# One slot per buffer, slack in the planner's ready times, and a new order for a linear-attention and two-MLP kernel

## The chip, the cores and the metric

One core of one Trainium2 chip runs the whole program in one launch. The metric is the device time of one execution in microseconds (us); lower is better. TensorE (PE) multiplies matrices, VectorE (DVE), ScalarE (ACT) and GpSimd (POOL) do the elementwise work, SyncE (SP) issues nearly all DMAs. Each engine works its own list of instructions in the order in which the program was written, and waits on semaphores where another engine or a DMA must come first.

## The reference, cut to what matters

```python
# q, k, v: (4, 8, 576, 64); w_phi: (64, 128); all float32
def phi(x):
    proj = np.einsum('bhsd,df->bhsf', x, w_phi)
    proj = proj - np.max(np.abs(proj), axis=-1, keepdims=True)
    return np.concatenate([np.exp(proj), np.exp(-proj)], axis=-1)
q_p, k_p = (phi(q), phi(k))
kv = np.einsum('bhsf,bhsd->bhfd', k_p, v)
z = np.sum(k_p, axis=2)
attn = np.einsum('bhsf,bhfd->bhsd', q_p, kv) / (np.einsum('bhsf,bhf->bhs', q_p, z)[..., None] + 1e-06)
x = attn.transpose(0, 2, 1, 3).reshape(2304, 512)
h = x @ w_in                        # (512, 2048)
x = (h * sigmoid(h)) @ w_out        # first MLP, (2048, 512)
h = np.maximum(x @ w_in2, 0.0)
out = (h * h) @ w_out2              # second MLP
```

## The kernel before

The program has three stages on PE. **Attention** goes by batch `j` (0 to 3) and pair of heads `p` (0 to 3): `keys_of` projects the keys, takes exponentials and builds the 129-row table `kv`; `queries_of(b, p)` does the same for half a batch of queries (`b`, 0 to 7), multiplies with `kv`, sends the denominators through DRAM to spread them over partitions (`rr`, `rd`, `qb`, three DMAs in a row) and writes the normalised result, split in a high and a low part, into the tiles `x`. **The first MLP** takes tokens in six pieces `i` (288, 288, four of 432 columns) and hidden units in 16 chunks `c`: `chunk(i, c)` makes 12 matmuls into a PSUM bank `h`, then ACT (`a`), DVE (`a`), ACT (`gh`) and DVE (`gl`) turn it into the gate, and 12 matmuls add to the four outputs `o`. Its weights come as raw 1 MB loads `wbits`; ACT and DVE make them float32 (`wc`, three instructions) and split them in high and low halves (`w`). Chunks in `STREAM` are stored to `w1d` and fetched again for every later piece. The second MLP's weights are converted in the same way during pieces 3 to 5: 32 loads `wr`, 32 conversions `wc` through the two slots of pool `c`, 32 stores to `w2d`. **The second MLP** works by Strassen-like products: `quad` (PE into `pa`, `pb`, `pc`) and `fold` (PE into `y`), with weights made by `w_sums` and `y_ahead`.

Nothing of this is issued in the order of the code. Each piece of work is recorded by `op(key, engine, cost, ...)`, and `Plan.run` (L176 to L265) plays the program through with its own costs: on every engine the ready operation with the smallest `key` starts, a DMA takes a fixed issue time, a latency and a rate (L84), an operation becomes ready at the end of its last input plus an entry of `LAT` (L260). The order in which operations start in this play is the order in which they are emitted. The numbers in `KEYS` (L290) shift the keys of whole groups: when weights are loaded, when queries of a batch come, and so on. Buffers are counted by pool (`self.free`), and a tile is allocated when its first operation is emitted, from a pool with one tag and several `bufs`; only five pools carry a slot number (`homes`, a heap that gives the lowest free number), and there it only chooses between two memory regions. Where the play leaves PE idle for more than 1.9 us in the attention, `idle_mm` puts in small matmuls (L1563, L1573).

Of the kernel before, what the change touches and what calls it, by code (L numbers as in the profile page):

```python
# [75 lines left out]
class Plan:  # L76
# [3 lines left out]
        "PE": {"ACT": 200, "DVE": 200, "POOL": 280, "SP": 250}, "ACT": {"DVE": 142, "PE": 170, "POOL": 200, "SP": 140},  # L80
        "DVE": {"ACT": 120, "PE": 150, "POOL": 170, "SP": 120}, "POOL": {"ACT": 135, "DVE": 135, "PE": 150, "SP": 150},
# [94 lines left out]
    def run(self):  # L176
# [9 lines left out]
        while left:  # L186
            moved = True
            while moved:
                moved = False
# [47 lines left out]
            while events and events[0][0] <= now:  # L237
# [5 lines left out]
                for b in o.frees:  # L243
                    b.users -= 1
                    if not b.users:
                        self.free[b.pool] += 1
                        if b.pool in self.homes:
                            heapq.heappush(self.homes[b.pool], b.home)
                        if b.pool in self.last:
                            last = self.last[b.pool]  # L250
# [50 lines left out]
def attention_then_two_mlps(ctx, tc, kT, qT, v, w_phi, w1, w2, out):  # L301
# [69 lines left out]
    def slot(name, unit, shape=(128, S), dt=F32):  # L371
        if unit.early:
            return Buf("e", lambda: ep[0].tile(list(shape), dt, tag="t", name=name), unit)
        b = Buf("t", None, unit)

        def make():
            if b.home < NT:
                return tp.tile(list(shape), dt, tag="t", bufs=NT, name=name)
            late_pool()
            return ep[2].tile(list(shape), dt, tag="t", bufs=NTL, name=name)  # L380
# [18 lines left out]
    def g_tiles(late, dts, name):  # L399
        return Buf(  # L400
            late or "g",
            lambda: [
                (late_pool() if late else gp).tile([128, LB], dt, tag=t, bufs=1 if late else 2, name=t + name)
                for t, dt in zip(("a", "gh", "gl"), dts)
            ], None
        )

    def wide(pool_, shape, dt, name):
        b = Buf(pool_, None, None)

        def make():
            wide_pool()
            if pool_ == "x7":
                return [
                    [late_pool().tile([128, w], dt, tag=t, bufs=1, name=name + t)[:, :QB] for t, w in (("gl", LB), ("xx", QB))],
                    [cp.tile([128, QB], dt, tag="c", bufs=2, name=f"{name}c{x}") for x in range(2)],
                ]
            if pool_ == "xt":
# [10 lines left out]
            return [sp.tile([128, LB], dt, tag="o", bufs=2, name=f"{name}{x}") for x in range(2)]  # L429
# [58 lines left out]
    blank_u = Buf("e", lambda: ep[0].tile([128, 256], F32, tag="t", name="zeros"), None)  # L488
    blank_ps = Buf("eb", lambda: psb.tile([128, 512], F32, tag="b", name="warm"), None)
# [63 lines left out]
    def w_tile(layer, c, turn=0):  # L553
        if (layer, c, turn) not in wch:
            shape, dt = [128, 4, 512], F32R
            if layer in (1, 3) and c < 2:
                wch[layer, c, turn] = Buf(
                    "wl", lambda: wide_pool().tile([128, 8, 256], F32R, tag="w", bufs=2, name=f"wl{layer}_{c}"), None
                )
# [6 lines left out]
            wch[layer, c, turn] = Buf(  # L566
                "w" if first else "wq",
                lambda: (wp if first else late_pool()).tile(
                    shape, dt, tag="w", bufs=NC - NW if first else NWQ, name=f"w{layer}_{c}_{turn}"
                ), None  # L570
# [1053 lines left out]
```

## Time and profile before

| what | value |
|---|---|
| median of 3 runs (961.84 to 964.12) | 962.52 us |
| the profiled execution, its own time | 966.88 us |
| its span from the first to the last instruction | 965.1 us |
| PE busy in the span | 936.1 us, 97% |
| DVE, ACT, POOL busy | 655.4, 558.3, 149.7 us |
| DMA traffic | 175.86 MB, mean 182 GB/s |
| chain that ended last, by engine | PE 70%, DMA 13%, DVE 10%, ACT 4% |

The page gives busy time by engine over the whole span and in 40 slices; the windows view gives the same for stretches of one's choice; the chain is followed back from the last instruction, at each step to what released it. A wait is put down to the semaphore that came last.

### The profile page before, as it was taken

How to read it: one execution, taken by the hardware profiler on the slowest of the kernel's cores; microseconds unless marked ns; L12 is line 12 of the kernel's file. 1: busy time of each engine (PE TensorE's matmuls, PEld its weight loads, DVE VectorE, ACT ScalarE, POOL GpSimd, SP SyncE). 2: the span in 40 equal slices, each digit the busy share in tenths (PEclk: the TensorE clock that was granted, in tenths of full speed). 3: DMA queues.
4: the chain of work that ended last, by engine and by line, in shares of the span. 5: the costliest groups of instructions: out<-in, count | busy, mean ns of one | idle time of the engine just before them, and what ended most of it. 6: DMA issues, size and time to landing. Idle time of an engine off the chain costs nothing.

```text
span 965.1 us, 16758 instructions
## 1 busy us (share of the span) xinstructions
PE 936.1 (97%) x6210; PEld 896.5 (93%) x6210; DVE 655.4 (68%) x1137; ACT 558.3 (58%) x1191; POOL 149.7 (16%) x160
## 2 busy tenths in 40 slices
PE   9889999999999999999999999999999999999998
PEld 7569999999999999988899899999999999999998
DVE  6889996646754477547554855757466799897952
ACT  7967786777766567434333554546565675444431
POOL 4210230200400203000001333511100430000000
PEclk9989999999999999999999999999999999999999
DMA  9769537344353145798878563444237574544422
GB/s 322 228 226 341 192 111 209 99 147 155 103 160 122 33 149 173 235 315 263 294 276 280 180 251 105 170 166 164 108 126 247 197 284 134 173 133 118 156 78 66
DMA packets 83954, 175.86 MB, mean 182 GB/s; under 512 B 14880, under 2 KB 43680, under 8 KB 77216
## 3 DMA queue, kind: packets, MB, share of 16 engines
q1 hardware_dynamic: 83728, 174.72, 54.7%
q8 instruction: 49, 0.80, 0.3%
q14 instruction: 33, 0.27, 0.1%
q10 hardware_dynamic: 144, 0.07, 0.0%
HBM read 126.11 MB, written 48.57 MB: 181 GB/s over the span
## 4 chain that ended last, share of the span: by engine, by line
PE 70%; DMA 13%; DVE 10%; ACT 4%; issue 2%; SPq 1%; DVEq 0%; ACTq 0%
PE y L1420 17%; PE h L1080 13%; PE o L1119 13%; PE pb L1248 7%; DMA w2d<-wc 5%; PE pa L1248 5%; PE pc L1248 5%; PE pkv L843 4%; PE pn L999 3%; DMA qb<-rd 2%; DMA qr<-qT 1%; DVE wc L537 1%; DVE w L449 1%; PE pk L775 1%; ACT wc L528 1%
## 5 line engine op out<-in xcount | busy, mean ns | idle before, releaser
L1080 PE MATMUL h<-x,w 128*128 128x432 f32 (+1 forms) x1152 | 214.2, 339 | 4.9 <-ACT x L445 2.1
L1119 PE MATMUL o<-gh,w 128*128 128x432 f32 (+1 forms) x768 | 209.7, 340 | 1.8 <-ACT gh L445 1.8
L1080 PEld LDWEIGHTS h<-x,w 128*128 128x128 f32 x1152 | 197.6, 189 | 12.8 <-ACT x L445 2.3
L1119 PEld LDWEIGHTS o<-gh,w 128*128 128x128 f32 x768 | 140.0, 188 | 7.6 <-ACT gh L445 3.1
L1119 PE MATMUL o<-gl,w 128*128 128x432 f32 (+1 forms) x384 | 130.9, 341 | 3.9 <-DVE gl L449 3.9
L947 POOL PARTITION_ALL_REDUCE qm<-qp x32 | 71.7, 2266 | 176.5 <-ACT qp L940 139.7
L1119 PEld LDWEIGHTS o<-gl,w 128*128 128x128 f32 x384 | 72.1, 188 | 9.6 <-DVE gl L449 7.5
L449 DVE TENSOR_TENSOR gl<-a,gh 128x432 fp32r<-128x432 f32 (+1 forms) x96 | 56.9, 593 | 29.9 <-ACT gh L445 29.0
L648 POOL TENSOR_TENSOR ws<-ws 128x256 f32<-128x256 f32 x52 | 48.5, 934 | 155.9 <-DVE w L449 103.2
L445 ACT CAST gh<-a 128x432 fp32r<-128x432 f32 (+1 forms) x96 | 49.5, 516 | 38.4 <-DVE a L1088 37.9
L1088 DVE SCALAR_TENSOR_TENSOR a<-a,h 128x432 f32<-128x432 f32 (+1 forms) x96 | 52.7, 549 | 26.1 <-ACT a L1084 25.7
L1084 ACT ACTIVATE a<-h 128x432 f32<-128x432 f32 (+1 forms) x96 | 47.4, 493 | 21.4 <-PE h L1080 21.3
L535 DVE TENSOR_SCALAR wc<-wc 128x512 int32<-128x512 int32 (+1 forms) x48 | 25.8, 537 | 43.8 <-ACT wc L528 43.5
L528 ACT ACTIVATE wc<-wr 128x512 f32<-128x512 f32 x32 | 21.3, 666 | 51.3 <-DMA w2d<-wc 43.1
L843 PE MATMUL pkv<-v,kd 128*128 128x128 f32 x256 | 49.6, 275 | 0.8 <-issue 0.8
L843 PE MATMUL pkv<-v,ke 128*128 128x128 f32 x256 | 49.5, 275 | 0.0
L965 ACT ACTIVATE qe<-qp 128x576 f32<-128x576 f32 x64 | 41.8, 686 | 9.1 <-DVE qp L953 8.8
L449 DVE TENSOR_TENSOR qo<-qe,qh 128x576 fp32r<-128x576 f32 x48 | 37.9, 800 | 11.7 <-ACT qh L445 10.8
L1420 PE MATMUL y<-yb,w 128*128 128x256 f32 x316 | 44.3, 279 | 1.4 <-DVE yb L449 1.4
L999 PE MATMUL pn<-qh,kv 128*65 128x288 f32 x192 | 42.4, 295 | 0.6 <-ACT qn L1002 0.6
L1420 PEld LDWEIGHTS y<-yb,w 128*128 128x128 f32 x316 | 40.1, 188 | 1.6 <-DVE yb L449 1.6
L843 PEld LDWEIGHTS pkv<-v,kd 128*128 128x128 f32 x256 | 39.5, 192 | 1.9 <-issue 1.0
(373 smaller groups left out, 2278.6 us busy)
## 6 DMA issues: line engine op xcount, KB each, us to landing
w<-w1d SPq DMA_DIRECT2D x30, 1024.0 KB, 5.6
wbits<-w SPq DMA_DIRECT2D x16, 1024.0 KB, 7.9
wr<-w SPq DMA_DIRECT2D x32, 512.0 KB, 5.2
fold<-gd SPq DMA_DIRECT2D x32, 512.0 KB, 3.9
gd<-g SPq DMA_DIRECT2D x24, 384.0 KB, 2.3
w2d<-wc SPq DMA_DIRECT2D x32, 256.0 KB, 5.3
qr<-qT SPq DMA_DIRECT2D x56, 144.0 KB, 4.3
ws<-w2d SPq DMA_DIRECT2D x26, 256.0 KB, 4.6
```

Source lines behind the costliest of these rows:

```text
L445: nc.scalar.copy(out=dst, in_=src)
L449: e.tensor_tensor(out=dst, in0=src, in1=hi.bitcast(F32), op=ALU.subtract)
L648: nc.gpsimd.tensor_tensor(out=get(f)[:, o], in0=get(f)[:, a], in1=get(f)[:, b], op=how)
L843: nc.tensor.matmul(get(ps)[:, o:o + 128], feats[a](s)[:, t], get(vt)[:, c:c + 128], start=t == 0 and a == 0 and s == 0, stop=False, skip_g ...
L947: nc.gpsimd.partition_all_reduce(get(mx), get(pr).rearrange("p a t -> p (a t)"), 128, bass.bass_isa.ReduceOp.absmax)
L999: nc.tensor.matmul(get(ps)[:D1, :HB], w, get(e)[:, t], start=x == 0, stop=x == len(ops) - 1)
L1080: nc.tensor.matmul(get(ps)[:, :cols], a, x[:, cc, :cols], start=k == 0, stop=k == 3 * ND - 1)
L1084: nc.scalar.activation(out=get(gb)[0][:, :cols], in_=get(ps)[:, :cols], func=AF.Tanh, scale=0.5)
L1088: nc.vector.scalar_tensor_tensor(out=a, in0=a, scalar=1.0, in1=get(ps)[:, :cols], op0=ALU.add, op1=ALU.mult)
L1119: nc.tensor.matmul(get(acc)[:, :cols], a, g[:, :cols], start=c == 0 and x == 0, stop=c == NC - 1 and x == 2)
L1248: nc.tensor.matmul(get(ps)[:, :QB], ws[a][:, f], row(b, y, cc), start=first and k == 0, stop=k == 5, skip_group_check=True,)
L1420: nc.tensor.matmul(get(acc)[:, d * 256:d * 256 + half], get(ws[a][0])[:, ws[a][1], s], both(y)[:, j], start=q == 0 and d == 0 and x == 0, ...
```

## The change

Three things are changed. **Slots.** Every pool now has a queue of slot numbers (a `deque`); planning takes the slot at the front and puts a freed one at the back, so a buffer gets the slot that has been free the longest, and the tile is made under a tag of its own (`t3`, `b5`) with `bufs=1`. PSUM banks get numbers in the same way. **Slack.** An operation that waits for another engine becomes ready later in the play: by `md` = 524 ns after a DMA, `mp` = 304 ns where PE waits for another engine, `me` = 50 ns otherwise; nothing is added on one and the same engine, and `LAT` has new entries for ACT and DVE with themselves. **Order.** All numbers of `KEYS` are others; `bx` goes from 8 to 6, which moves two more pairs of keys (6 and 7) to the form in which ACT makes the exponential out of PSUM with a bias, without the subtraction on DVE, and `nwr` from 4 to 2, the number of chunks by which a raw weight load may run ahead of the split. The program has the same matmuls but for four more `idle_mm` ones, six subtractions fewer on DVE, 30 instructions more on ACT (36 small exponentials from PSUM and 6 negations for 12 exponentials of whole groups), and ten more stores of `gd`, since more of its tiles lie in two parts.

```diff
     LAT = {
-        "PE": {"ACT": 200, "DVE": 200, "POOL": 280, "SP": 250}, "ACT": {"DVE": 142, "PE": 170, "POOL": 200, "SP": 140},
-        "DVE": {"ACT": 120, "PE": 150, "POOL": 170, "SP": 120}, "POOL": {"ACT": 135, "DVE": 135, "PE": 150, "SP": 150},
+        "PE": {"ACT": 200, "DVE": 200, "POOL": 280, "SP": 250}, "ACT": {"ACT": 115, "DVE": 142, "PE": 170, "POOL": 200, "SP": 140},
+        "DVE": {"DVE": 122, "ACT": 120, "PE": 150, "POOL": 170, "SP": 120}, "POOL": {"ACT": 135, "DVE": 135, "PE": 150, "SP": 150},
...
-        self.homes = {p: list(range(32)) for p in ("t", "xt", "gq", "fx", "rb")}
+        self.homes = {p: deque(range(n)) for p, n in pools.items()}
+        self.opened = dict(pools)
...
-                        if b.pool in self.homes:
-                            b.home = heapq.heappop(self.homes[b.pool])
+                        b.home = self.homes[b.pool].popleft()
...
-                        if b.pool in self.homes:
-                            heapq.heappush(self.homes[b.pool], b.home)
+                        self.homes[b.pool].append(b.home)
...
-                    a.ready = max(a.ready, now + self.LAT[o.engine].get(a.engine, 20 if a.engine == "ACT" else 0))
+                    slack = KEYS["md"] if o.engine == "SP" else KEYS["mp"] if a.engine == "PE" != o.engine else KEYS["me"]
+                    if o.engine == a.engine:
+                        slack = 0
+                    a.ready = max(a.ready, now + self.LAT[o.engine].get(a.engine, 0) + max(0, slack))
...
 KEYS = {
-    "k0s": 15.71, "q0s": 16.3, "q0": 9.87, "w0": 53.89, "ws": 10.28, "we": -9.07, "Q1": 45.24, "A1": 1.22, "Q2":
...
+    "k0s": 19.81, "q0s": 16.62, "q0": 10.46, "w0": 164.39, "ws": 74.59, "we": -0.62, "Q1": 44.46, "A1": -7.97,
...
+    "ss": 32.21, "md": 524, "mp": 304, "me": 50,
...
-        return Buf(pool_, lambda: psb.tile([128, 512], F32, tag="b", name=name), unit)
+        b = Buf(pool_, None, unit)
+
+        def make():
+            home, base = b.home, {"eb": 0, "acc": 0, "att": 4, "h": 4 + NATT}
+            opens = plan.source["pb"] if pool_ == "pb" else ()
+            at = base[opens[home]] + opens[:home].count(opens[home]) if opens else base[pool_] + home
+            return psb.tile([128, 512], F32, tag=f"b{at}", bufs=1, name=name)
...
+    def homed(pool_, name, where, shape, dt, tag, unit=None):
+        b = Buf(pool_, None, unit)
+        b.make = lambda: where().tile(list(shape), dt, tag=f"{tag}{b.home}", bufs=1, name=name)
+        return b
...
-            f = Buf("c", lambda: cp.tile([128, cols], F32, tag="c", name="wc" + n), None)
+            raw = homed("raw", "wr" + n, lambda: rp, (128, 2 * cols), I32, "raw")
+            f = homed("c", "wc" + n, lambda: cp, (128, cols), F32, "c")
```

Three places show the new order. The names end in numbers: `qb0_2` is block 0, pair 2; `w0_5` chunk 5 of the first MLP; `wc1_2_1` chunk 2, second half, of the second MLP's weights.

SP before the first chunk of the first MLP, before:

```order
L1025 DMA qb0_1_546<-rd_101 64x576
L1016 DMA rr0_2_550<-qn0_2_514 96x1x6
L522 DMA wbits_7_0_576<-w1 128x2048
L1025 DMA qb1_0_596<-rd_101 64x576
L1016 DMA rr0_3_599<-qn0_3_583 96x1x6
L597 DMA w1d_99<-w0_4_0_585 128x2048
L1022 DMA rd_101<-rr0_2_550 96x6
L1022 DMA rd_101<-rr0_3_599 96x6
L1016 DMA rr1_1_659<-qn1_1_635 96x1x6
L1025 DMA qb0_2_663<-rd_101 64x576
L1025 DMA qb0_3_674<-rd_101 64x576
```

The same place on SP in the change:

```order
L1037 DMA qb0_0_498<-rd_101 64x576
L1028 DMA rr0_2_500<-qn0_2_486 96x1x6
L1037 DMA qb0_1_520<-rd_101 64x576
L541 DMA wbits_4_0_539<-w1 128x2048
L1028 DMA rr0_3_542<-qn0_3_529 96x1x6
L541 DMA wbits_5_0_565<-w1 128x2048
L1034 DMA rd_101<-rr0_2_500 96x6
L1034 DMA rd_101<-rr0_3_542 96x6
L1028 DMA rr1_0_610<-qn1_0_589 96x1x6
L1037 DMA qb0_2_615<-rd_101 64x576
L1037 DMA qb0_3_629<-rd_101 64x576
```

The raw load `wbits_7` stands ahead of `qb0_3` before, `wbits_5` is the last one there now; of block 1 `rr1_0`, `rr1_1` and `qb1_0` stood ahead of it before, `rr1_0` alone now.

DVE around the last two normalisations of block 0 (`x0_2`, `x0_3`), before:

```order
L449 TENSOR_TENSOR w0_5_0_671<-wc0_5_0_548,w0_5_0_671 128x2x512
L1041 TENSOR_TENSOR x0_2_690<-qn0_2_514,qb0_2_663 64x288 x2
L1019 RECIPROCAL rr1_1_659<-rr1_1_659 96x6
L1041 TENSOR_TENSOR x0_3_695<-qn0_3_583,qb0_3_674 64x288 x2
L449 TENSOR_TENSOR x_0_533<-x0_2_690,x_0_533 128x288
```

The same place on DVE in the change:

```order
L468 TENSOR_TENSOR w0_2_0_537<-wc0_2_0_502,w0_2_0_537 128x2x512
L468 TENSOR_TENSOR w0_3_0_563<-wc0_3_0_527,w0_3_0_563 128x2x512
L965 TENSOR_TENSOR qp1_3_608<-qp1_3_608,qm1_3_631 128x576
L1031 RECIPROCAL rr1_0_610<-rr1_0_610 96x6
L1053 TENSOR_TENSOR x0_2_654<-qn0_2_486,qb0_2_615 64x288 x2
L1053 TENSOR_TENSOR x0_3_662<-qn0_3_529,qb0_3_629 64x288 x2
L468 TENSOR_TENSOR x_0_569<-x0_2_654,x_0_569 128x288
```

Six weight splits (`w0_0` to `w0_5`) are written ahead of `x0_2` before, four (`w0_0` to `w0_3`) now.

ACT in piece 4 of the first MLP, before:

```order
L445 CAST gh4_2_5424<-a4_2_5423 128x432
L528 ACTIVATE wc1_1_1_5444<-wr1_1_1_5329 128x512
L528 ACTIVATE wc1_2_1_5472<-wr1_2_1_5351 128x512
L528 ACTIVATE wc1_3_1_5495<-wr1_3_1_5428 128x512
L1084 ACTIVATE a4_3_5510<-h4_3_5478 128x432
L445 CAST gh4_3_5511<-a4_3_5510 128x432
L1084 ACTIVATE a4_4_5535<-h4_4_5497 128x432
L445 CAST gh4_4_5536<-a4_4_5535 128x432
L1084 ACTIVATE a4_5_5545<-h4_5_5521 128x432
L528 ACTIVATE wc1_4_1_5552<-wr1_4_1_5458 128x512
```

ACT in the same piece in the change:

```order
L547 ACTIVATE wc1_4_1_5726<-wr1_4_1_5675 128x512
L1096 ACTIVATE a4_10_5734<-h4_10_5713 128x432
L464 CAST gh4_10_5735<-a4_10_5734 128x432
L464 CAST x_5_5063<-x7_2_5771 128x288
L547 ACTIVATE wc1_5_1_5779<-wr1_5_1_5738 128x512
L1096 ACTIVATE a4_11_5786<-h4_11_5756 128x432
L464 CAST gh4_11_5787<-a4_11_5786 128x432
L1096 ACTIVATE a4_12_5820<-h4_12_5802 128x432
L547 ACTIVATE wc1_6_1_5832<-wr1_6_1_5781 128x512
```

Three conversions in a row stood between two chunks' gates; now there is one per chunk, and the 32 of them begin some four chunks later and reach from chunk 8 of piece 3 to chunk 12 of piece 5 (before: to chunk 14 of piece 4). PE's own list went from groups of three (three `h`, then three `o`) to one `h` and one `o` in turn, and the last block of queries (`b` = 7) from piece 3 into piece 4.

## Rows read from the trace of the kernel before

**Rows 1.** The page: the span, and PE's busy time.

```profile
span 965.1 us, 16758 instructions
...
PE 936.1 (97%) x6210; PEld 896.5 (93%) x6210; DVE 655.4 (68%) x1137; ACT 558.3 (58%) x1191; POOL 149.7 (16%) x160
```

**Rows 2.** Windows: length, busy time per engine, PE clock, DMA share, GB/s.

```profile
0.00:25.00 25.00, 22.84 (x166) 18.00 (x168) 16.64 (x26) 19.59 (x42) 9.80 (x18) 1.00 0.92 322
25.00:50.00 25.00, 20.39 (x135) 14.74 (x136) 20.52 (x30) 21.93 (x42) 6.95 (x9) 0.95 0.72 229
50.00:75.00 25.00, 20.93 (x128) 16.66 (x127) 22.56 (x38) 16.93 (x31) 2.59 (x7) 0.85 0.68 230
75.00:100.00 25.00, 25.00 (x216) 24.43 (x215) 24.40 (x44) 18.60 (x34) 0.45 (x6) 1.00 0.98 329
100.00:150.00 50.00, 49.57 (x381) 48.74 (x380) 46.45 (x73) 42.04 (x87) 13.64 (x6) 1.00 0.41 138
...
400.00:450.00 50.00, 47.90 (x240) 44.59 (x240) 30.59 (x62) 19.62 (x41) 0.00 (x0) 1.00 0.87 292
450.00:500.00 50.00, 47.98 (x241) 44.66 (x240) 26.88 (x50) 19.47 (x36) 0.00 (x0) 1.00 0.77 261
500.00:550.00 50.00, 47.71 (x239) 44.29 (x238) 30.30 (x45) 23.42 (x41) 10.74 (x11) 1.00 0.73 246
550.00:600.00 50.00, 50.00 (x258) 48.02 (x259) 30.17 (x45) 22.69 (x41) 17.41 (x22) 1.00 0.49 173
...
750.00:800.00 50.00, 46.94 (x321) 46.21 (x320) 43.05 (x66) 32.26 (x61) 18.96 (x19) 1.00 0.66 232
```

**Rows 3.** The chain that ended last, 30 to 60 us: start, us, what.

```profile
34.31 5.66 DMA rd<-rr
...
39.98 8.30 DMA qb<-rd
...
50.51 1.72 DVE qp L953
...
53.01 2.29 ACT qe L965 x4
...
55.35 3.90 DMA qb<-rd
```

**Rows 4.** Timelines of PE and ACT in the same stretch: start, us, [idle before <-releaser].

```profile
22.84 2.10 PE L999 MATMUL pn<-qe,kv 128*65 128x288 f32 x8
...
41.91 2.25 PE L999 MATMUL pn<-qe,kv 128*65 128x288 f32 x8 [1.67 <-ACT kv L858]
...
64.13 0.41 ACT L1084 ACTIVATE a<-h 128x288 f32<-128x288 f32 x1 [1.02 <-PE h L1080]
```

**Rows 5.** Groups by line, 0 to 100 us: busy us, mean ns.

```profile
L537 DVE SCALAR_TENSOR_TENSOR wc<-wbits,wc 128x1024 int32<-128x1024 int32 x13 | 15.9, 1223 | 0.4
...
L449 DVE TENSOR_TENSOR w<-wc,w 128x1024 fp32r<-128x1024 f32 x11 | 13.6, 1238 | 2.5 <-ACT w L445 2.5
...
L805 DVE TENSOR_TENSOR kd<-pk,mx 128x512 f32<-128x512 f32 (+1 forms) x21 | 11.5, 556 | 0.5
...
L535 DVE TENSOR_SCALAR wc<-wc 128x1024 int32<-128x1024 int32 x13 | 9.0, 695 | 0.0
```

**Rows 6.** Tile qb, 0 to 110 us: from issue to landing.

```profile
DMA to landing us min/median/max: 3.0/5.0/9.2
```

**Rows 7.** Waits, 350 to 560 us: us in total, times, longest.

```profile
ACT wc L528 <- DMA w2d<-wc: 43.1, 20, 4.3
```

**Rows 8.** Timelines of ACT and PE, 473 to 481 us.

```profile
473.63 0.66 ACT L528 ACTIVATE wc<-wr 128x512 f32<-128x512 f32 x1 [4.31 <-DMA w2d<-wc]
476.87 0.66 ACT L528 ACTIVATE wc<-wr 128x512 f32<-128x512 f32 x1 [2.58 <-DMA w2d<-wc]
...
479.87 0.46 PE L1119 MATMUL o<-gh,w 128*128 128x432 f32 x1 [1.14 <-ACT gh L445]
```

**Rows 9.** Tile w2d, whole span: from issue to landing.

```profile
DMA to landing us min/median/max: 2.0/5.3/9.9
```

More of the change, by code (lines that the diff above doesn't have):

```diff
@@ L1 @@
 import heapq
+from collections import deque
 from contextlib import ExitStack
@@ L372, in slot @@
         if unit.early:
-            return Buf("e", lambda: ep[0].tile(list(shape), dt, tag="t", name=name), unit)
+            b = Buf("e", None, unit)
+            b.make = lambda: ep[0].tile(list(shape), dt, tag=f"t{b.home}", bufs=1, name=name)
+            return b
         b = Buf("t", None, unit)
@@ L377, in make @@
             if b.home < NT:
[L378 removed]
+                return tp.tile(list(shape), dt, tag=f"t{b.home}", bufs=1, name=name)
             late_pool()
[L380 removed]
+            return ep[2].tile(list(shape), dt, tag=f"t{b.home}", bufs=1, name=name)
         b.make = make
@@ L399, in g_tiles @@
     def g_tiles(late, dts, name):
[L400 to L406, printed above, removed]
+        b = Buf(late or "g", None, None)
+        b.make = lambda: [
+            (late_pool() if late else gp).tile([128, LB], dt, tag=t if late else f"{t}{b.home}", bufs=1, name=t + name)
+            for t, dt in zip(("a", "gh", "gl"), dts)
+        ]
+        return b
     def wide(pool_, shape, dt, name):
@@ L415, in make @@
                     [late_pool().tile([128, w], dt, tag=t, bufs=1, name=name + t)[:, :QB] for t, w in (("gl", LB), ("xx", QB))],
-                    [cp.tile([128, QB], dt, tag="c", bufs=2, name=f"{name}c{x}") for x in range(2)],
+                    [cp.tile([128, QB], dt, tag=f"c{x}", bufs=1, name=f"{name}c{x}") for x in range(2)],
                 ]
@@ L420, in make @@
                 return [
-                    lp[not near].tile(list(shape), dt, tag="xt" + x, bufs=XTL if near else NXT - XTL, name=name + x)
-                    for x in "hl"
+                    lp[not near].tile(list(shape), dt, tag=f"xt{x}{b.home}", bufs=1, name=name + x) for x in "hl"
                 ]
@@ L428, in make @@
                 return [late_pool().tile([128, LB], dt, tag=t, bufs=1, name=name + t) for t in ("a", "gh")]
-            return [sp.tile([128, LB], dt, tag="o", bufs=2, name=f"{name}{x}") for x in range(2)]
+            return [sp.tile([128, LB], dt, tag=f"o{x}", bufs=1, name=f"{name}{x}") for x in range(2)]
         b.make = make
@@ L565, in w_tile @@
             first = c // 2 in (1, 2, 4, 6) if layer in (1, 3) else c in IN_W and not turn
[L566 to L570, printed above, removed]
+            wch[layer, c, turn] = homed(
+                "w" if first else "wq", f"w{layer}_{c}_{turn}", (lambda: wp) if first else late_pool, shape, dt, "w"
             )
@@ L652, in w_sums @@
         hi, lo = ([b for b, *_ in w_runs(layer, q, x, 0, 7)] for x in range(2))
-        f = Buf("raw", lambda: rp.tile([128, 4, 256], F32, tag="raw", name=f"ws{layer}_{q}"), None)
+        f = homed("raw", f"ws{layer}_{q}", lambda: rp, (128, 4, 256), F32, "raw")
         W = ("ws" if layer == 1 else "ys", q)
@@ L781, in keys_of @@
         feats, done = [], []
-        mxs = [Buf("mx", lambda g=g: sp.tile([128, 2, 4], F32, tag="mx", bufs=4, name=f"mx{n}_{g}"), None) for g in range(3)]
+        mxs = [homed("mx", f"mx{n}_{g}", lambda: sp, (128, 2, 4), F32, "mx") for g in range(3)]
         ds = [[slot(f"kd{n}_{a}", u, (128, NKT, F)), slot(f"ke{n}_{a}", u, (128, NKT, F))] for a in range(2)]
@@ L1033, in queries_of @@
         late = b > 0 and p % 2
-        x = Buf(
-            "xy" if late else "xx",
-            lambda: (late_pool() if late else sp).tile([128, QB if late else HB], F32, tag="xx", bufs=1 if late else 2, name="x" + n)[:, :HB], None
-        )
+        x = Buf("xy" if late else "xx", None, None)
+        x.make = lambda: (late_pool() if late else sp).tile(
+            [128, QB if late else HB], F32, tag="xx" if late else f"xx{x.home}", bufs=1, name="x" + n
+        )[:, :HB]
         def mul():
@@ L1366, in make @@
                     if plan.source["rb"][t.home] == "x7":
-                        return [cp.tile([128, 2, 256], F32R, tag="c", name=f"yb{n}{y}") for y in range(2)]
-                    b = rp.tile([128, 2, 2, 256], F32R, tag="raw", name=f"yb{n}")
+                        return [cp.tile([128, 2, 256], F32R, tag=f"c{y}", bufs=1, name=f"yb{n}{y}") for y in range(2)]
+                    b = rp.tile([128, 2, 2, 256], F32R, tag="raw2", bufs=1, name=f"yb{n}")
                     return [b[:, 0], b[:, 1]]
@@ L1433, in fold @@
             return
-        ab, cb = (
-            Buf("ev", lambda x=x: rp.tile([128, 2, 2, 256], F32, tag="raw", name=f"ye{i}_{x}"), None) for x in range(2)
-        )
+        ab, cb = (homed("ev", f"ye{i}_{x}", lambda: rp, (128, 2, 2, 256), F32, "raw") for x in range(2))
         s1, u2, u4, c12 = ((lambda x=x, b=b: get(b)[:, x, :, :half]) for x in range(2) for b in (ab, cb))
```

32 lines of the change are left out of this document (16 added, 16 removed), and 9 rows, old and new, of the table KEYS.

## The prediction

> **What bounds the kernel now.** I read the page first. PE is busy for 936.1 of 965.1 us [rows 1], and the change takes no matmul away, so all that an order can win on PE lies in its 29.0 us of idle time and in stretches at the lower clock. The windows show where these lie [rows 2]. From 75 us to 150 PE is as good as full (25.00 of 25, 49.57 of 50). Three places are not. From 25 to 75 us, ahead of and around the first chunk of the first MLP, PE idles 4.61 + 4.07 = 8.7 us, and the granted clock is 0.95 and 0.85: with its two levels, 1.2 and 2.4 GHz, a mean of 0.95 and 0.85 over 25 us loses up to 1.25 + 3.75 = 5.0 us of work. Together 13.7 us. From 400 to 550 us, in pieces 3 to 5 of the first MLP, PE idles 2.10 + 2.02 + 2.29 = 6.4 us. From 750 to 800 us, where the second MLP passes from quads to folds, it idles 3.1 us. The rest is the start, the end and single gaps.
>
> Then the waits. In the first place the chain names three DMAs that carry the denominators: a store `rd` of 5.66 us and two broadcasts `qb` of 8.30 and 3.90 us [rows 3]. The product `pn0_3` of the last pair of block 0 ends at 41.91 + 2.25 = 44.2 us, and the first gate comes only at 64.1 us, when the chunk `h0_0` has all four pairs of `x` [rows 4]. In the second place ACT waits for the store `w2d` 20 times, 43.1 us in all [rows 7]: a conversion needs one of two slots of pool `c`, and the slot is free when its store has landed. One pair of such waits is in the rows: 4.31 and 2.58 us on ACT, with nothing behind them on ACT begun meanwhile, and PE then waits 1.14 us for `gh` of ACT [rows 8].
>
> **The change part by part.**
>
> *Slots and slack.* Neither is an instruction. A slot that has been free the longest can only take a wait for its last user away or leave it; no row of before is such a wait on PE that I can name, so I put it at nothing by itself. The slack only moves operations apart in the play; on the chip an operation still starts when its inputs are there. Its cover is that another matmul is ready; where none is, the order is the same as without it.
>
> *The head.* Block 0 goes first now: in PE's list `pq1_0` and `pn1_0` have gone behind `pn0_3`. `pn1_0` is 8 records like the row of 2.10 us [rows 4], and the 1.67 us that PE waited for `kv` on ACT, behind a weight conversion, may go too. So `pn0_3` ends at 44.2 - 2.1 = 42.1 us, or at 40.4 us without the wait. Behind it come the spread `rr0_3`, the reciprocal, the store `rd` and the broadcast `qb0_3`. I price each of the first two DMAs between 3.0 us, the shortest landing of a `qb` [rows 6], and the 5.66 us of the store [rows 3], and give 2 to 3 us for ACT, DVE and SP between them: 8 to 14 us. The broadcast takes 3.0 to 5.0 us [rows 6]; normalising, splitting and the second half of `h0_0` another 2.5. That is 40.4 + 8 + 3 + 2.5 = 53.9 us at best and 42.1 + 14 + 5 + 2.5 = 63.6 at worst for the point that was at 64.1 us. I take 58 us, 6 earlier, near the middle, because SP's list helps and hinders: two raw loads of 1 MB fewer stand ahead of `qb0_3` (the 8.30 us of `qb0_1` were spent with several of them under way), but `qb0_2` stands behind `rr1_0`, and so behind the product `pn1_0`.
>
> What is late next is the weights. Four splits instead of six stand ahead of the last `x` on DVE. One costs 0.695 + 1.223 + 1.238 = 3.16 us there [rows 5], two 6.3 us, which now come behind the first chunk. The six subtractions that `bx` takes away give 6 x 0.556 = 3.3 us back [rows 5]. DVE is busy for 24.40 of 25 us from 75 to 100 us and for 46.45 of 50 after it, so it has little room there, but it has 8.4 + 4.5 + 2.4 = 15.3 us of idle time before 75 us [rows 2]. ACT pays for the exponentials from PSUM; it is busy for 18.60 of 25 and 42.04 of 50 us [rows 2], so I take it as hidden, and if that cover goes it is as late as DVE. I take 1 us off for these: **5 us gained**, with ends of 9 us gained and, if all 3.0 us of net DVE work comes onto PE and `x` is not earlier, 3 us lost. The four `idle_mm` more, 8 records of 0.26 us each by the 2.10 us row [rows 4], fill a wait that the play foresees; outside it they would cost 2 us.
>
> *The conversions of the second MLP's weights.* Before, up to four stand in a row on ACT; now nearly every one has a chunk's gate between it and the next. A chunk of 432 columns is 24 matmuls; the windows hold 240 in 47.90 us [rows 2], so a chunk takes 4.8 us and a slot comes round after two, 9.6 us. A store lands after 5.3 us in the median, 9.9 at most [rows 9], and the conversion before it takes ACT 0.66 us [rows 8] and DVE under 2; 8 us are mostly enough. So the waits of 43.1 us should go for the most part, and with them the PE idle time that they cause. Not all 6.4 us are theirs, and five conversions and the last queries move into stretches that had none: 550 to 600 us had no idle time at all. **4.5 us gained**, with ends of 6.4 and 0.
>
> By the Trainium skill ("DMA: Bandwidth & Descriptors", section "Anatomy of one DMA — SWDGE (gpsimd) path") a DMA costs some 2.0 us and its bytes at 436 GB/s. For 256 KB that is, as an estimate, 2.6 us, a slot would nearly always be back in time, and this term would be 0. The median of 5.3 us and the 43.1 us of waits speak against it here; 2.0 us is only the shortest of the 32 landings.
>
> *The passage to the folds.* Product 6 of the last quad goes two groups of matmuls earlier, so its slots of `xt` come free earlier for the folds; the ten more stores of `gd` lie on SP, which no wait of PE names. PE idles 3.1 us from 750 to 800 us [rows 2]. **0.5 us gained**, between 3 gained and 2 lost, since new keys may open a wait here as well as close one.
>
> Sum: 5 + 4.5 + 0.5 = 10 us. The profiled execution took 966.88 us, 1.78 us of it outside the span; it would take 956.9. It lies 4.4 us above the median of 962.5, so the forecast for the median is 952.5 us.
>
> **The rivals.**
>
> *The weights become the bound (slower).* DVE cannot make up the splits that now come late. Three chunks late are 9.5 us, less the 3.3 given back 6.2; ACT's new exponentials lie on the same path; the early `x` is of no use without weights; and the block of queries pushed into piece 4 fills ACT and DVE where the conversions were to find room, so nothing is won there either. It decides where PE reaches a chunk between `h0_5` and `h0_9` before DVE has split its weights. For it: DVE's 24.40 of 25 us. Against it: DVE's idle time before 75 us, and PE has `h0_0` to `h0_4`, four `o` and two key projections to do first. About 5 us lost: 967.5 us.
>
> *The head alone.* The store is not what costs PE at 400 to 550 us, or other waits of ACT take its place. 5 us and a little: 957. The rule of the Trainium skill named above ("DMA: Bandwidth & Descriptors") would give this case.
>
> *The conversions alone.* The head's gain is eaten by DVE, and the 4.5 us stay: 958.
>
> *The change doesn't do what it says.* Slots and slack take no wait away that counts, the gaps only move: within 1 us of 962.5.
>
> **How the numbers follow.** The forecast, from 6 to 16 us gained, has a chance of 0.54, the head alone 0.12, the conversions alone 0.12, no effect 0.10, the weights as bound 0.12. About 0.2%, 1.9 us, is what a measurement of this kernel can tell from no change. Faster is the first three, 0.78; same 0.10; slower 0.12. The range goes from 946 us (9 + 6.4 + 1 gained) to 961.5: it leaves out the slower rival, half of no effect and a few in a hundred below.
>
> **What would show it.** In the profile after: the first gate `a<-h` at about 58 us and a clock nearer 1 between 25 and 75 us; PE idle there under 6 us; DVE as full as before from 75 to 150 us, and PE still over 99%. From 350 to 600 us ACT's wait for `w2d` under 15 us and PE idle under 3 us. From 750 to 800 us nearly as before. I am wrong in the head if PE waits for DVE `w` between `h0_5` and `h0_9`, and wrong in the second place if the waits of ACT fall and PE's idle time there doesn't.

## The result and the profile after

The changed kernel takes 952.88 us (median of 4 executions, 952.76 to 953.66), the kernel before 963.32 us beside it (median of 4, 961.84 to 967.03). The ratio is 0.9888, with a 95% interval from 0.9858 to 0.9917: 1.1% faster. The forecast was 952.5 us.

The page of the changed kernel, as [rows 1] for before: the span, and PE's busy time.

```profile
span 951.1 us, 16767 instructions
...
PE 935.2 (98%) x6218; PEld 896.2 (94%) x6218; DVE 645.5 (68%) x1131; ACT 565.7 (59%) x1221; POOL 154.9 (16%) x160
```

PE's busy time is what it was, with eight records more; its idle time fell from 29.0 us to 951.1 - 935.2 = 15.9. The windows say where. They answer to [rows 2], but for PE alone; columns are the stretch, its length, PE busy (records), the granted clock, DMA share, GB/s.

```profile
...
25.00:50.00 25.00, 22.82 (x132) 1.00 0.64 228
50.00:75.00 25.00, 23.26 (x158) 1.00 0.74 239
75.00:100.00 25.00, 24.87 (x211) 1.00 0.90 304
100.00:150.00 50.00, 49.16 (x384) 1.00 0.60 206
...
400.00:450.00 50.00, 49.77 (x260) 1.00 0.81 278
450.00:500.00 50.00, 48.37 (x258) 1.00 0.71 229
500.00:550.00 50.00, 49.82 (x254) 1.00 0.75 261
...
750.00:800.00 50.00, 49.44 (x376) 1.00 0.67 222
```

From 25 to 75 us PE is idle for 3.9 us instead of 8.7, and in this execution the clock stays at its upper level, where the mean was 0.95 and 0.85. From 400 to 550 us it idles 2.0 us instead of 6.4, from 750 to 800 us 0.6 instead of 3.1.

Windows of a time cut the work of two orders differently, so I also counted what PE lost: for each record the time to the start of the next one, less the mean of its kind in the changed kernel (the slowest tenth left out of that mean), summed by stage. E8, below, has the same lists as before and a time that can't be told from it; its profiled execution (963.24 us) is nearer to the median than that of before (966.88 us), which lies 4.4 us above it.

| PE time lost, us | 0 to 150 | 150 to 400 | 400 to 600 | 600 to 750 | 750 to 800 | span |
|---|---|---|---|---|---|---|
| before, profiled | 22.8 | 5.2 | 10.3 | 2.5 | 4.0 | 965.1 |
| E8 (lists of before) | 22.6 | 4.2 | 7.3 | 2.6 | 4.1 | 961.2 |
| after | 18.4 | 3.4 | 4.4 | 1.5 | 1.3 | 951.1 |

So 4.2 us of the gain lie in the head, 0.8 between it and 400 us, 2.9 in the stretch of the conversions (5.9 against the profiled execution of before, of which 3.0 were its own), 1.1 in the quads, 2.8 at the passage to the folds. That is 11.8 us. The eight records more are `idle_mm` matmuls, which take 1.16 us at 42.94 us of the span (the 0.26 us a record of [rows 4] is that of another matmul, `pn`). So 10.6 us are left, and the spans differ by 10.1.

### The profile page after: what moved, and what is told of

Same layout as the page of the kernel before. It is cut to its first block, busy times and chain, and to the rows that moved or that the text cites. A ratio compares the mean times of both kernels' runs of the same rounds, so it can differ in the third digit from the quotient of the medians.

```text
span 951.1 us, 16767 instructions
## 1 busy us (share of the span) xinstructions
PE 935.2 (98%) x6218; PEld 896.2 (94%) x6218; DVE 645.5 (68%) x1131; ACT 565.7 (59%) x1221; POOL 154.9 (16%) x160
## 4 chain that ended last, share of the span: by engine, by line
PE 82%; DMA 6%; DVE 6%; ACT 2%; POOL 2%; issue 1%; SPq 1%; DVEq 0%; ACTq 0%; POOLq 0%
PE o L1131 18%; PE h L1092 18%; PE y L1432 17%; PE pb L1260 7%; PE pkv L855 6%; PE pc L1260 5%; PE pa L1260 5%; PE pn L1011 4%; DMA wr<-w 3%; POOL qm L959 2%; PE pk L787 1%; DMA qr<-qT 1%; DMA gd<-g 1%; DMA w2d<-wc 1%; PE pkv L862 1%
## 5 line engine op out<-in xcount | busy, mean ns | idle before, releaser
L1092 PE MATMUL h<-x,w 128*128 128x432 f32 (+1 forms) x1152 | 217.0, 337 | 0.0
L1131 PE MATMUL o<-gh,w 128*128 128x432 f32 (+1 forms) x768 | 213.3, 339 | 0.2 <-ACT gh L464 0.2
L959 POOL PARTITION_ALL_REDUCE qm<-qp x32 | 77.1, 2438 | 243.9 <-ACT qp L952 149.7
L468 DVE TENSOR_TENSOR gl<-a,gh 128x432 fp32r<-128x432 f32 (+1 forms) x96 | 60.2, 627 | 17.9 <-ACT gh L464 17.0
L662 POOL TENSOR_TENSOR ws<-ws 128x256 f32<-128x256 f32 x52 | 45.8, 883 | 139.4 <-DVE w L468 83.3
L977 ACT ACTIVATE qe<-qp 128x576 f32<-128x576 f32 x64 | 41.3, 683 | 10.1 <-DVE qp L965 10.0
L464 ACT CAST yb<-fold 128x512 fp32r<-128x512 f32 x26 | 16.1, 620 | 51.6 <-PE y L1432 51.4
L1275 DVE TENSOR_TENSOR glq<-pb,aq 128x384 f32<-128x384 f32 x24 | 13.3, 556 | 40.5 <-PE pb L1260 40.5
```

The source lines that it names most:

```text
L464: nc.scalar.copy(out=dst, in_=src)
L468: e.tensor_tensor(out=dst, in0=src, in1=hi.bitcast(F32), op=ALU.subtract)
L662: nc.gpsimd.tensor_tensor(out=get(f)[:, o], in0=get(f)[:, a], in1=get(f)[:, b], op=how)
L959: nc.gpsimd.partition_all_reduce(get(mx), get(pr).rearrange("p a t -> p (a t)"), 128, bass.bass_isa.ReduceOp.absmax)
L1092: nc.tensor.matmul(get(ps)[:, :cols], a, x[:, cc, :cols], start=k == 0, stop=k == 3 * ND - 1)
L1131: nc.tensor.matmul(get(acc)[:, :cols], a, g[:, :cols], start=c == 0 and x == 0, stop=c == NC - 1 and x == 2)
```

## Experiments

**The two halves of the change, apart.** An order can be kept while the allocation changes, since the play doesn't depend on which slot a buffer gets. E1 has the lists of before with the slots of the change, E2 the lists of the change with the rotating pools of before. Only SP's stores of `gd` differ, since the slots decide which of its tiles lie in two parts: 12 more in E1 and E8 than before, 8 fewer in E2 than in the change. Each version was timed beside executions of the kernel before, whose median lay between 961.8 and 963.3 us. No version was timed beside the changed kernel, so a difference between those two is uncertain by some 1.5 us more; the ratios to the kernel before are not.

E1, against the changed kernel (`LAT` and the table as before, too):

```diff
...
-                    a.ready = max(a.ready, now + self.LAT[o.engine].get(a.engine, 0) + max(0, slack))
+                    a.ready = max(a.ready, now + self.LAT[o.engine].get(a.engine, 20 if a.engine == "ACT" else 0))
...
-    "k0s": 19.81, "q0s": 16.62, "q0": 10.46, "w0": 164.39, "ws": 74.59, "we": -0.62, "Q1": 44.46, "A1": -7.97,
+    "k0s": 15.71, "q0s": 16.3, "q0": 9.87, "w0": 53.89, "ws": 10.28, "we": -9.07, "Q1": 45.24, "A1": 1.22, "Q2":
```

> The slots of the change alone: every engine works the very list of the kernel before (same planner costs, same key table, no slack); only the tile that a buffer gets is another. Theory A (the order carries the whole gain, slots nothing, as the prediction put it): 962.5 to 964.5 us, ratio to before 0.999 to 1.001, PE idle time of the span 28 to 30 us. Rival B (slots take real waits for tiles away): 957 to 960 us, and waits on ACT or DVE fall that the kernel before has.

Measured: 970.51 us against 961.88, ratio 1.0097 (1.0071 to 1.0124). Neither theory had it: the slots alone make the kernel 8.6 us slower.

E2, against the kernel before:

```diff
+                    slack = KEYS["md"] if o.engine == "SP" else KEYS["mp"] if a.engine == "PE" != o.engine else KEYS["me"]
...
+                    a.ready = max(a.ready, now + self.LAT[o.engine].get(a.engine, 0) + max(0, slack))
...
+    "ss": 32.21, "md": 524, "mp": 304, "me": 50,
```

> The other half: the key table, the slack and the planner's entries of the change, so every engine works the list of the changed kernel, but buffers come from the rotating pools of the kernel before. Theory A: 952 to 954 us, ratio 0.988 to 0.990. Rival B: 955 to 960 us, with waits on PE, ACT or DVE that the changed kernel does not have.

Measured: 950.76 us, ratio 0.9883 (0.9858 to 0.9909), against 0.9888 with slots. The order carries the whole gain; on it the slots cost nothing that these intervals can tell.

**Which slots cost.** E7 gives only the PSUM banks fixed slots, E8 only the tiles in SBUF; the lists are those of before.

E7, against the kernel before:

```diff
-        return Buf(pool_, lambda: psb.tile([128, 512], F32, tag="b", name=name), unit)
...
+            return psb.tile([128, 512], F32, tag=f"b{at}", bufs=1, name=name)
```

> The kernel before, every engine's list unchanged, with the slots of the change for the eight PSUM banks alone: each pool of banks (att, h, acc, eb) keeps to its own banks, where before any pool takes any bank of the eight. The slots together cost 8.6 us on this order. Theory P (it is the banks: a matmul group waits for the readers of the very bank that its pool freed): 967 to 971 us. Rival Q (it is the tiles in SBUF): 960 to 964 us.

E8, against E1:

```diff
...
-            return psb.tile([128, 512], F32, tag=f"b{at}", bufs=1, name=name)
...
+        return Buf(pool_, lambda: psb.tile([128, 512], F32, tag="b", name=name), unit)
```

> The same with the slots for the tiles in SBUF alone, banks as before. Theory P: 960 to 964 us. Rival Q: 967 to 971 us. If both come out between, the two costs add up.

Measured: E7 971.20 us, ratio 1.0092 (1.0057 to 1.0127); E8 961.33 us, ratio 0.9990 (0.9969 to 1.0012), both against 961.78. It is the banks (theory P). PE's waits over the whole span, in E7 and then in E8 (engine and line, waited for: us, times, longest):

```profile
PE pq L945 <- ACT kd L837: 3.1, 2, 2.7
PE h L1100 <- DVE a L1108: 3.0, 3, 1.4
```

```profile
PE o L1119 <- DVE gl L456: 2.8, 6, 0.8
PE pn L999 <- ACT qe L965: 2.7, 1, 2.7
```

The first two are waits for whoever reads the bank that the group is to write: `kd` reads the bank of `pk`, and `pq` and `pk` both take theirs from the two banks of pool `att`; `a` on DVE reads `h`. In E8 the largest waits are for inputs. The same place on PE's timeline, E7 and then E8 (start, length, [idle before <-releaser]):

```profile
172.37 0.29 PE L1139 MATMUL o<-gh,w 128*128 128x288 f32 x1
175.33 0.61 PE L945 MATMUL pq<-ql,wst_lo 128*128 128x288 f32 x1 [2.67 <-ACT kd L837]
```

```profile
171.66 0.29 PE L1119 MATMUL o<-gh,w 128*128 128x288 f32 x1
171.79 0.30 PE L925 MATMUL pq<-ql,wst_lo 128*128 128x288 f32 x1
```

PE waits 2.67 us for a bank that, with eight banks shared, it need not have taken, and after this wait the window from 150 to 200 us of E7 has a mean clock of 0.97.

```profile
150.00:200.00 50.00, 46.82 (x357) 0.97 0.55 161
```

**Slack and table, apart.** E3 is the changed kernel without slack, E4 with slack and the old table, E12 with nearly the same slack. All three have the slots of the change, the banks' too.

E3:

```diff
-    "ss": 32.21, "md": 524, "mp": 304, "me": 50,
+    "ss": 32.21, "md": 0, "mp": 0, "me": 0,
```

> The changed kernel with md, mp and me at zero: same key table, same slots, but the play takes inputs as there without slack. Theory A' (the table carries the gain, slack hardly matters): 952 to 955 us, ACT's wait for w2d from 340 to 580 us stays under 15 us. Rival S (without slack the play starts work too early, so that what it sets in a row waits on the chip): 956 to 962 us, PE idle 4 to 8 us more than the 15.9 us of the changed kernel, spread over many short gaps.

Measured: 967.48 us, ratio 1.0066 (1.0041 to 1.0090), 14.6 us above the changed kernel: more than rival S had. A' is right on one point: ACT's conversions wait for `w2d` 1.8 us, three times, over the whole span. The loss is spread as S had it; two of its windows:

```profile
400.00:450.00 50.00, 48.03 (x242) 0.97 0.80 274
...
750.00:800.00 50.00, 46.62 (x315) 1.00 0.65 227
```

E4:

```diff
-    "k0s": 19.81, "q0s": 16.62, "q0": 10.46, "w0": 164.39, "ws": 74.59, "we": -0.62, "Q1": 44.46, "A1": -7.97,
+    "k0s": 15.71, "q0s": 16.3, "q0": 9.87, "w0": 53.89, "ws": 10.28, "we": -9.07, "Q1": 45.24, "A1": 1.22, "Q2":
...
+    "ss": 44.05, "md": 524, "mp": 304, "me": 50,
```

> The changed kernel with the 57 old numbers of the key table (bx 8 and nwr 4 among them) and the new slack. Theory A': 961 to 965 us, the place of 25 to 75 us as in the kernel before (PE idle 8 to 9 us, clock 0.95 and 0.85), ACT's wait for w2d over 30 us. Rival S: 955 to 959 us, with PE idle at 400 to 550 us under 3 us.

Measured: 974.69 us, ratio 1.0153 (1.0113 to 1.0194), slower than either theory. Two windows and ACT's wait from 340 to 600 us:

```profile
400.00:450.00 50.00, 46.31 (x222) 0.97 0.83 278
...
750.00:800.00 50.00, 50.00 (x328) 1.00 0.74 252
```

```profile
ACT wc L547 <- DMA w2d<-wc: 39.9, 19, 5.2
```

E4 and E1 differ by the slack and the new entries of `LAT`, the changed kernel and E3 by the slack alone. From 750 to 800 us, where the passage to the folds lies, PE idles 0.0 us in E4 and 2.5 in E1, 0.6 in the changed kernel and 3.4 in E3. E4 is late there, and its one gap behind the quads, 0.39 us, comes at 808 us; that changes little. At this place the slack helps, with either table. The wait for `w2d` is the other way round: 39.9 us in E4 and 39.2 in E1, 10.3 in the changed kernel and 1.8 in E3. That one belongs to the table. In all, slack with the old table gains nothing: E4 is no faster than E1, which has the same slots (974.69 and 970.51 us, with ratios whose intervals overlap).

E12:

```diff
-    "ss": 32.21, "md": 524, "mp": 304, "me": 50,
+    "ss": 32.21, "md": 500, "mp": 304, "me": 50,
```

> The changed kernel with 500 ns of slack after a DMA for 524; the play comes out otherwise in places (4244 of 4571 rows of PE stay). Theory S (the slack is a mechanism, and 24 ns don't matter): 951 to 955 us. Rival T (the table was fitted to one play, and any other play of it loses): 957 to 968 us, as without slack, with the loss in short gaps all over.

Measured: 953.11 us, ratio 0.9911 (0.9875 to 0.9947). Theory S: the table isn't fitted to one play so closely that 24 ns and some 300 moved rows of PE lose the gain.

**The head.** E5 was to measure what the chain of denominators costs there.

```diff
+            if b == 0:
+                nc.sync.dma_start(out=rd[b * NP + p, 0:128], in_=eps[:, 0])
+                return
...
+                in_=(rd[b * NP + p] if b else v[0, 0, 0:576]).partition_broadcast(D)
```

> The kernel before, every engine's list unchanged, but for block 0 the store rd takes a constant and the broadcast qb reads a row of v, so x of block 0 no longer waits for the reciprocals to go out and come back (the normalisation of block 0 is left out). Theory H (x is what PE waits for between 25 and 75 us, as the head term has it): the first gate 6 to 10 us earlier than 64.1 us, PE idle from 25 to 75 us under 5 us, 954 to 958 us against 962. Rival W (weights and DVE are next at once): x is early, h0_1 to h0_8 are not, 960 to 963 us.

Measured: 973.89 us, ratio 1.0119 (1.0078 to 1.0160). It took the chain away and put slower broadcasts in its place. The four `qb` and three others from 20 to 85 us, and DVE's wait for them, in E5:

```profile
DMA to landing us min/median/max: 3.4/8.8/15.6
```

```profile
DVE x L1045 <- DMA qb<-v: 12.1, 3, 5.0
```

In before the same stretch has:

```profile
DMA to landing us min/median/max: 3.0/3.9/9.2
```

```profile
DVE x L1041 <- DMA qb<-rd: 3.9, 3, 1.5
```

So it can't tell H from W. What it shows is the reverse of its question: the last broadcast of block 0 lands at 69.8 us instead of 59.6, PE's work is 11 us later at 75 us (the same records matched in both traces), and the time is 12 us longer. Why a broadcast of a row of `v` takes so long to land I didn't settle. The stores of the constant, which the edit also put in, are slow too: the four land after 8.3 to 13.7 us.

E11 takes the load keys back:

```diff
-    ... "w0": 164.39, "ws": 74.59, "we": -0.62, ... "nwr": 2,
+    ... "w0": 53.89, "ws": 10.28, "we": -9.07, ... "nwr": 4,
```

> The changed kernel with the four numbers that place the raw loads and splits of the first MLP's weights as before (w0, ws, we, nwr 4); the order is laid anew from there. Theory L (fewer raw loads under way make the head better): the clock drops between 40 and 70 us come back, PE idle from 25 to 75 us from 3.9 to 7 us or more, 956 to 960 us. Rival M (the head is better by the order of its keys and queries alone): clock 1.0, PE idle under 5 us there, any loss is elsewhere; 952 to 955 us if the rest of the order is as good.

Measured: 960.91 us, ratio 0.9978 (0.9956 to 1.0001): theory L by its signs, though 0.9 us above the range it gave. Windows of E11, and one of PE's waits from 30 to 75 us:

```profile
25.00:50.00 25.00, 21.22 (x118) 14.52 (x117) 23.39 (x28) 22.61 (x38) 10.60 (x10) 0.94 0.66 224
50.00:75.00 25.00, 20.31 (x120) 15.90 (x119) 18.93 (x34) 14.33 (x30) 3.01 (x1) 0.92 0.53 178
```

```profile
PE h L1092 <- ACT x L464: 2.7, 1, 2.7
```

PE idles 8.5 us from 25 to 75 us, the clock drops are back, and `h` waits for `x` as in the kernel before.

**The conversions.** E6 keeps the lists of before and lets the stores read another tile:

```diff
-            nc.sync.dma_start(out=w2d[c, :, part * 512:(part + 1) * 512], in_=get(f))
+            nc.sync.dma_start(out=w2d[c, :, part * 512:(part + 1) * 512], in_=get(wch[0, 15, 0])[:, part].bitcast(F32))
```

> The kernel before, every engine's list unchanged, but the 32 stores w2d, of the same size, read a resident weight tile and not the conversion's tile (so the second MLP gets other weights, which is what is left out); the slot of pool c is free when DVE is done with it. Theory C (the wait for the store costs PE the idle time of 400 to 550 us): ACT's wait for w2d gone, PE idle there from 6.4 to under 3 us, 957 to 959.5 us against 962. Rival K (another wait takes its place, the raw load wr or the gates): ACT waits for wr instead, PE idle over 4.5 us, 960.5 to 962.5 us.

Measured: 956.46 us, ratio 0.9947 (0.9923 to 0.9971), 5.3 us less than before. Windows of E6, and below them of E8, which has the wait (44.8 us, 20 times):

```profile
400.00:450.00 50.00, 50.00 (x257) 1.00 0.91 308
450.00:500.00 50.00, 50.00 (x258) 1.00 0.87 295
500.00:550.00 50.00, 49.67 (x255) 1.00 0.69 234
```

```profile
400.00:450.00 50.00, 48.66 (x244) 1.00 0.88 296
450.00:500.00 50.00, 48.51 (x244) 1.00 0.84 272
500.00:550.00 50.00, 48.85 (x247) 1.00 0.74 250
```

Theory C, 0.5 us below its range: without the wait nearly all of PE's idle time of 4.0 us there is gone, with as much DMA traffic. By the count above PE loses 0.8 us from 400 to 550 us, where E8 loses 7.1, and 1.8 us more than E8 from 550 to 600 us. ACT waits 13.5 us for the raw loads `wr` instead (8.2 before), and PE doesn't feel it.

E10, in the changed kernel:

```diff
-    1.68, "ks": -3.38, "w2a": 55.02, "w2b": 1.35, "bx": 6, "pe": 41.86, "el": 330.56, "wl": -5.23, "kl": 7.34,
+    1.68, "ks": -3.38, "w2a": 61.15, "w2b": 1.05, "bx": 6, "pe": 41.86, "el": 330.56, "wl": -5.23, "kl": 7.34,
```

> The changed kernel with the two numbers that place the conversions of the second MLP's weights as before (w2a 61.15, w2b 1.05 for 55.02 and 1.35), so they stand closer together; PE's list is nearly the same (4549 of 4571 rows). Theory C (their spacing is what took the wait for the store away): ACT's wait for w2d from 10 back to over 25 us, PE idle from 400 to 550 us from 2.0 to 4 us or more, 955 to 958 us. Rival S (the slack after a DMA keeps them apart anyway): wait under 15 us, 952 to 954 us.

Measured: 956.05 us, ratio 0.9939 (0.9921 to 0.9957), 3.2 us above the changed kernel. ACT's wait from 340 to 580 us:

```profile
ACT wc L547 <- DMA w2d<-wc: 20.2, 16, 3.5
```

It doubles, PE's idle time from 400 to 550 us is 2.9 + 2.0 + 0.0 = 4.9 us instead of 2.0, and from 450 to 500 us the mean clock is 0.97. Theory C again, though the wait stays under the 25 us that it named.

**The folds.** E9 takes four keys back:

```diff
-    1.46, "yb": 2.3, "yl": -67.46, "yw": 0.52, "p1": -38.15, "p2": -0.91, "q1s": 4.33, "ee": 26.01, "e1": 91.11,
+    -0.65, "yb": 19.88, "yl": 68.18, "yw": 4.25, "p1": -38.15, "p2": -0.91, "q1s": 4.33, "ee": 26.01, "e1": 91.11,
```

> The changed kernel with four numbers of its table as before (ya, yb, yl, yw: loads and sums of the folds' weights); PE's list stays the same, ACT's, DVE's and SP's change in the second MLP alone. Theory F (these numbers carry the gain at the passage to the folds): PE idle from 750 to 800 us back from 0.6 to 2.5 us or more, 955 to 957 us. Rival G (it comes from elsewhere, the order of PE or the play with slack): 952 to 954 us.

Measured: 957.48 us, ratio 0.9951 (0.9931 to 0.9971). Theory F missed the time by 0.5 us, and the place: these keys cost 4.6 us, but earlier. Windows of E9:

```profile
500.00:550.00 50.00, 48.80 (x248) 46.02 (x247) 34.20 (x52) 24.48 (x43) 11.98 (x12) 1.00 0.83 284
...
600.00:650.00 50.00, 48.39 (x276) 47.75 (x275) 34.68 (x57) 29.98 (x58) 19.39 (x19) 1.00 0.47 169
750.00:800.00 50.00, 49.63 (x368) 49.26 (x366) 39.68 (x73) 33.34 (x65) 9.36 (x10) 1.00 0.65 221
```

At the passage PE idles 0.4 us, as in the changed kernel. From 500 to 550 us it idles 1.2 us (0.2 in the changed kernel), from 600 to 650 us 1.6 us (none there, 1.7 before) and from 650 to 700 us 1.1 us (0.4). One of these waits on PE's timeline, and DVE's work ahead of it:

```profile
648.87 0.45 PE L1260 MATMUL pb<-xt_3h,w 128*128 128x384 f32 x1 [1.24 <-DVE glq L1275]
```

```profile
647.68 0.68 DVE L468 TENSOR_TENSOR yd<-ya,yd 128x512 fp32r<-128x512 f32 x1
648.27 0.55 DVE L1275 TENSOR_TENSOR glq<-pb,aq 128x384 f32<-128x384 f32 x1
```

A split of the folds' weights, `yd`, stands right ahead of the gate `glq`; in the changed kernel it is done at 637 us, well ahead of that gate. The kernel before has a wait of the same kind (`pb` for `glq`, 1.7 us).

## Why the prediction was right, and where it wasn't

**The forecast** of 952.5 us was hit to 0.4 us, and 10.4 us were gained where 10 were summed. That the sum is so close is in part luck. By the count of E8 and the changed kernel the three terms of 5, 4.5 and 0.5 us measured 4.2, 2.9 and 2.8, and 1.9 us came from stretches that the sum left out.

**The subtraction.** The sum took idle time of the profiled execution for idle time of the median. Of the 4.4 us by which that execution lay above the median, 3.0 stood in the very stretch of the conversions (10.3 us lost, 7.3 in E8). From profile to profile the change took 966.88 - 952.98 = 13.9 us, not 10; from median to median 10.4.

**The head** was put at 5 us and gave 4.2 to 4.4. The size held, the picture by half. The first gate was to come at 58 us:

```profile
L1096 ACT ACTIVATE a<-h x2: 403/404/404, 62.3 to 63.9; 128x288 f32<-128x288 f32 x2
```

It comes at 62.3, 1.8 us earlier than in [rows 4], not 6. As far as the broadcast the sum went right: `pn0_3` ends at 38.97 + 2.15 = 41.1 us (42.1 or 40.4 there), `qb0_3` goes out 10.7 us later (8 to 14) and lands after 3.6 us, at 55.4, where it landed at 59.6 before. The last term was mis-sized: from that landing to the gate it gave 2.5 us, and 6.9 were needed. DVE has `qp` of block 1 ahead of the two normalisations and waits for POOL's `qm` until 56.1 us, and PE has the products of block 1 ahead of the first chunk.

```profile
38.97 2.15 PE L1011 MATMUL pn<-qe,kv 128*65 128x288 f32 x8 [0.48 <-ACT qp L952]
...
56.13 0.76 DVE L965 TENSOR_TENSOR qp<-qp,qm 128x576 f32<-128x576 f32 x1 [2.03 <-POOL qm L959]
56.90 1.82 DVE L1053 TENSOR_TENSOR x<-qn,qb 64x288 f32<-64x288 f32 x4
```

What `x` being ready earlier bought was not an early gate but a gate without holes: PE does more queries first and then runs the first chunk and the second in one go.

```profile
57.66 2.24 PE L1011 MATMUL pn<-qe,kv 128*65 128x288 f32 x8 [0.39 <-ACT qe L977]
59.52 3.57 PE L1092 MATMUL h<-x,w 128*128 128x288 f32 x24
```

Before, the first chunk began at 57.44 us and then had to wait for `x`:

```profile
57.44 1.17 PE L1080 MATMUL h<-x,w 128*128 128x288 f32 x6
60.70 0.40 PE L1080 MATMUL h<-x,w 128*128 128x288 f32 x1 [2.09 <-ACT x L445]
61.74 1.09 PE L1080 MATMUL h<-x,w 128*128 128x288 f32 x3 [0.64 <-DVE x L449]
```

In this execution the clock doesn't drop there either; the lower clock had cost up to 5.0 us of work [rows 2], as much as the whole term. That can't be put down to the change alone. Of its four executions two were granted a mean clock of 1.000 and two 0.998, and their times don't follow it; E9, whose lists are the same as far as 520 us, has a clock of 0.93 from 50 to 75 us and loses no more in the head. The broadcasts land after 3.7 us in the median (5.0 in [rows 6]), and E11, laid anew from the load keys on, puts these keys behind the gain: with the old ones, the holes are back, and two drops of the clock. The weights did not become the next bound: from 60 to 150 us PE waits nowhere for `w` and once, 0.8 us, for `gl` of DVE. Still it is 98.7% busy from 75 to 150 us, not over 99%, and loses 3.2 us there, where it lost 1.7.

**The conversions** were put at 4.5 us. The step holds: ACT's wait for `w2d` [rows 7] fell from 43.1 us to

```profile
ACT wc L547 <- DMA wr<-w: 22.3, 13, 3.8
...
ACT wc L547 <- DMA w2d<-wc: 10.3, 7, 4.1
```

(340 to 560 us), PE's idle time there from 6.4 to 2.0, and E6 and E10 show that the one makes the other. Part of it came back as a wait for the raw load, 22.3 us where it was 8.2; the 13.5 us of it in E6 cost PE hardly anything. The 32 stores now go out from 392.6 to 576.9 us, one in 5.9 us, where it was one in 4.4. At the median the term is 2.9 us, since 3.0 us of it were the profiled execution's own; all of the wait is worth 5.3 (E6; by its interval 2.8 to 7.4).

The landing time in the sum was read from a mixed row: [rows 9] counts the 32 loads of `w2d` with the 32 stores. The stores alone landed after 5.3 us in the median and 8.9 at most, not 9.9; in the changed kernel after 4.6 us, 8.6 at most. The page has the median:

```profile
w2d<-wc SPq DMA_DIRECT2D x32, 256.0 KB, 4.6
```

By the Trainium skill ("DMA: Bandwidth & Descriptors", section "Anatomy of one DMA — SWDGE (gpsimd) path") a store of this size was estimated at 2.6 us. That section's fit is for DMAs that GpSimd issues; these stores go out from SyncE. Their 4.6 us don't agree with it, and the rival that hung on this rule fell.

**The passage to the folds** was put at 0.5 us and gave 2.8. This term was mis-sized. I had looked in the keys for a reason and found product 6; E9 shows that the folds' keys don't matter there, and E3 and E4 that the slack does.

**Slots and slack at nothing** was the step that failed outright. That a slot free the longest "can only take a wait for its last user away or leave it" is true within one pool. The banks had been one pool of eight on the chip, whatever the plan counted; tied to `att`, `h`, `acc` and `eb` they add waits and 9 us of time on the old order (E7). And the slack changes no start on the chip, but it changes the lists: without it the same table is 14.6 us slower (E3). Slack alone isn't it either: with the old table it gains nothing (E4 against E1). That the bank slots are harmless on the new order (E2) fits with the 304 ns that the play now leaves ahead of each matmul that waits for another engine; an order without slack on rotating banks, which would show it, wasn't run.

**Not named at all:** about 1 us in the quads, from 600 to 750 us. It goes with the folds' keys (E9) or the slack (E3), and the old table with the slack has it too (E4): from the first quad to the last PE idles 0.8 us in the changed kernel, 2.7 in E9, 2.4 in E3, but 0.7 in E4 and 2.7 in E1.

No version ran clearly faster than the changed kernel; E2 and E12 can't be told from it.

## What to carry to other kernels

When a planner lays the order, its error is paid in the lists. Here a play with later transfers and hand-overs gave the better order, but only together with a table of keys that goes with it (E3, E4); whether another table would do as well without slack wasn't tried. Before tying buffers to slots, ask which pools shared memory until now: with eight shared banks PE found a free one where, with banks of each pool's own, it waited 2.67 us for one reader (E8, E7). And take a prediction's idle times from an execution that lies at the median, or say which of them may be that execution's own.

## What the runs showed of the hardware that I had not expected

A broadcast of 576 floats to 64 partitions took 8.8 us in the median, 15.6 at most, when four of seven read a row of `v` and went out without the wait for `rd`, against 3.9 and 9.2 us from `rd` in the same stretch before (E5); the cause is open.

A single hole on PE behind the head can cost more than its length. Windows of 5 us of E3 and then of E7 (E7's hole is the 2.67 us above):

```profile
426.00:431.00 5.00, 3.03 (x16) 1.00 0.71 271
431.00:436.00 5.00, 5.00 (x19) 0.66 0.72 224
```

```profile
170.00:175.00 5.00, 2.22 (x15) 1.00 0.65 148
175.00:180.00 5.00, 4.67 (x26) 0.66 0.35 147
```

After 2.0 and 2.8 us of idle time the mean clock of the next 5 us is 0.66, so up to another 1.7 us of work is lost at each place. From 45 to 55 us the changed kernel idles 2.5 us, in four gaps, and keeps its clock in this execution; E10, with the same lists there, idles 2.1 us and keeps it too, and E9 idles 1.8 us and has a mean clock of 0.66 from 50 to 55 us. What decides it, these rows don't show.

Executions of the kernel before spread from 956.4 to 965.3 us (26 of them beside E9 to E12), those of the changed kernel from 952.8 to 953.7 (4).
